# Regrouping the first casts and transposes and moving the sigmoid gates half a stage later, in a one-core recurrence and max-out kernel

## The chip, the cores and the metric

The kernel runs on one core of a Trainium2 chip. The metric is the device time of one execution in microseconds (us); several executions give a median. A profile shows one execution in detail; its "span" is about 2 us shorter than the device time of the same execution. In this kernel PE is the matrix engine, ScalarE (ACT in the profile) does sigmoids and evictions from PSUM, VectorE (DVE) the recurrence, GpSimd (POOL) issues the casting transfers, SyncE (SP) issues the transposing transfers and the stores.

## The reference, cut to what matters

```
def reference(x, f_logit, lower_bound, w1, w2, w_out):     # x: 4 x 6144 x 256
    sig = 1 / (1 + exp(-f_logit))
    f = lb + (1 - lb) * sig
    for t in range(S):                                     # recurrence over time
        h = f[:, t] * h + (1 - f[:, t]) * x[:, t];  y[:, t] = h
    y = y.reshape(24576, 256)
    return maximum(y @ w1, y @ w2) @ w_out                 # 256 -> 1024 -> 256
```

## The kernel before

The tokens are cut into 48 blocks of 512. Blocks 0 to 3 come in one by one (their "chunks" 0 to 3 are turned by PE). From then on two blocks make a pair and share one chunk of 1024 tokens: pair p uses chunk p + 2, so pair 2 uses chunk 4, pair 4 uses chunk 6. A chunk is first cast from float32 to bfloat16 into a scratch buffer in DRAM (two buffers per input, used in turn), then transposed by a transfer into on-chip memory. Each chunk has an f part and an x part.

```
def fetch(c, s):                       # cast a chunk: GpSimd issues
    nc.gpsimd.dma_start(out=scratch[s][c % NSCR], in_=src)

def cross(c):                          # transpose chunk c, then cast chunk c + 2
    for s in range(2):
        nc.sync.dma_start_transpose(out=dst, in_=scratch[s][c % NSCR])
        held[c, s] = dst
    if c + NSCR < NCHUNK:
        for s in range(2): pool_waits(held[c, s])    # GpSimd waits for the landing
        for s in range(2): fetch(c + NSCR, s)

def pair_gate(p, q):                   # one of the four sigmoids of a pair, on ScalarE
    nc.scalar.activation(out=u[:, h, cols], in_=held[c, 0][:, h, cols], func=Sigmoid)

def first_layer(j, fc):                # 2 matmuls of 512 columns into PSUM (two buffers) ...
    ...
    if fc % 2: nc.scalar.activation(out=r, in_=dT, func=Relu)   # ... evicted by ScalarE
```

The main program, cut. The place of each `pair_gate` in this text is its place in ScalarE's instruction stream:

```
for c in range(1, 6): fetch(c, 0); fetch(c, 1)        # chunks 4 and 5 among them
...
cross(4)
second_layer(0); ...
cross(5)
for fc in range(8):
    second_layer(1, fc); ...
    if fc % 2: pair_gate(2, fc // 2)                   # gates of pair 2: in front of block 2's Relus
for fc in range(8): first_layer(2, fc)
for fc in range(8):
    first_layer(3, fc); second_layer(2, fc)
    if fc % 2: pair_gate(3, fc // 2)
    ...
    if fc == 0: cross(6)
for p in range(2, 24):                                 # the stages, 16 slots each
    gates = {5: 0, 11: 1, 13: 2, 15: 3}
    for slot in range(16):
        first_layer(2 * p + slot // 8, slot % 8)       # Relu at every odd slot
        ... second layer of the pair before, vector steps of the pair after ...
        if slot == 2: cross(chunk of pair p + 3)
        if slot in gates: pair_gate(p + 2, gates[slot])
```

Of the kernel before, what the change touches and what calls it, by code (L numbers as in the profile page):

```python
# [18 lines left out]
def kernel(  # L19
# [76 lines left out]
    def fetch(c, s):  # L96
        b, t0, nt, _ = chunks[c]
        src = srcs[s][b, t0 : t0 + nt, :]
        if by_xbar(c, s):
            nc.gpsimd.dma_start(  # L100
                out=pieces(scratch[s][c % NSCR][:]), in_=pieces(src)
            )
        else:
            nat = inpool.tile([P, TB // P, D], BF16, name=("fT", "xT")[s])
            nc.gpsimd.dma_start(
                out=nat[:].rearrange("p i d -> p (i d)"),
                in_=src.rearrange("(p i) d -> p (i d)", p=P),
            )
            held[c, s] = nat
# [31 lines left out]
                    )  # L141
            raws[k, s] = dst[:].rearrange("p k i m -> p k m i")

    def cross(c):

        if c >= NCHUNK:
            return
        for s in range(2):
            dst = inpool.tile([P, KC, CH], BF16, name=("fT", "xT")[s])
            nc.sync.dma_start_transpose(out=dst[:], in_=scratch[s][c % NSCR][:])  # L150
            held[c, s] = dst
        if c + NSCR < NCHUNK:
            for s in range(2):
                pool_waits(held[c, s][:, 0, 0:1])
            for s in range(2):
                fetch(c + NSCR, s)

    def turn_steps(j):
        b, t0, nb, c, o = blocks[j]
# [50 lines left out]
    def drive(v, u, xT, cols):  # L210
        nc.vector.tensor_tensor(  # L211
            out=like(v[:, :, cols], xT), in0=like(u[:, :, cols], xT), in1=xT,
            op=ALU.mult,
        )
# [65 lines left out]
    def pair_scans(p):  # L280
        c = blocks[2 * p][3]
        new_mid(p + NBLK, ("ff", "v"))
        u, ff, v = (mids[p + NBLK, t] for t in ("u", "ff", "v"))
        for j in (2 * p, 2 * p + 1):
            ys[j] = ypool.tile([P, KC, TB], BF16, name="y")

        def driven(t):
            cols = slice(t * TB, (t + 1) * TB)
            return lambda: drive(v, u, held[c, 1][:, :, cols], cols)

        def scanned(t, h):
            return lambda: scan(2 * p + t, h, ff, v, t * TB)

        return {
            "decay": lambda: decay(ff, u, slice(0, CH)),
            "drive0": driven(0),
            "drive1": driven(1),
            **{f"scan{t}{h}": scanned(t, h) for t in range(2) for h in range(KC)},
        }
# [4 lines left out]
    om = const.tile([P, KC], FP32)  # L304
    nom = const.tile([P, KC], FP32)
    lbc = const.tile([P, KC], FP32)
    waited = const.tile([P, 1], FP32)
    warm = const.tile([P, 1], FP32)
    wob = wpool.tile([P, FC, D], BF16)
# [26 lines left out]
    def pool_waits(t):  # L336
        nc.gpsimd.tensor_copy(out=waited[:], in_=t)  # L337
# [164 lines left out]
    def sum2(p):  # L502
        sum_of(p, 2, quarter(p, 1, 1), sums[p, 3][:], ALU.subtract)
# [4 lines left out]
    def sum4(p):  # L508
        sum_of(p, 4, quarter(p, 0, 1), sums[p, 2][:], ALU.subtract)
# [106 lines left out]
    with tc.manual_schedule():  # L616
        nc.sync.dma_start(out=lbc[:], in_=lower_bound.rearrange("(h p) -> p h", p=P))
        nc.vector.tensor_copy(out=ident[:], in_=ident_f[:])
        nc.vector.tensor_scalar(
            out=om[:], in0=lbc[:], scalar1=-1.0, scalar2=1.0, op0=ALU.mult, op1=ALU.add  # L620
        )
        nc.vector.tensor_scalar_add(out=nom[:], in0=lbc[:], scalar1=-1.0)
        fetch_first(0)
        fetch_first(1)
        for g in range(NG):
            fetch_w(g)
        pool_waits(w2n[0][:, 0, 0:1])
        nc.gpsimd.dma_start(
            out=wob[:].rearrange("p (g q) c -> p g (q c)", g=NG),
            in_=moe_w_out.rearrange("(g p q) c -> p g (q c)", g=NG, q=NQ),  # L630
        )
        for c in range(1, 6):
            for s in range(2):
                fetch(c, s)
        nc.scalar.activation(out=warm[:], in_=om[:, 0:1], func=AF.Sigmoid)
        wt = ps_d.tile([P, 2, 2 * TB], BF16, name="dT")
        for q in range(8):
            nc.tensor.transpose(wt[:, 0, 0:P], ident[:], ident[:])
        first_bf16(0, 0, nc.vector.tensor_copy)
        first_bf16(0, 1, nc.vector.tensor_copy)  # L640
        first_turn(0)
        first_recurrence(0)
        first_bf16(1, 0, nc.scalar.copy)
        first_bf16(1, 1, nc.scalar.copy)
        first_turn(1)
        first_recurrence(1)
        for fc in range(2):
            make_wd(fc, 1)
        make_wd(2, 2)
        pts = [turn_w1(0), turn_w1(1)]  # L650
        for fc in range(2):
            first_layer(0, fc)
        for k in range(2):
            keep_w1T(k, pts[k])
        for fc in range(2, 4):
            first_layer(0, fc)
        make_wd(4, 2)
        make_wd(6, 2)
        pts = [turn_w1(2), turn_w1(3)]
        for fc in range(4, 8):  # L660
            first_layer(0, fc)
        for k in range(2):
            keep_w1T(2 + k, pts[k])
        make_w13()
        turn(turn_steps(1))
        recurrence(1)
        cross(4)
        for fc in range(FC):
            second_layer(0, fc)
        turn(turn_steps(2))  # L670
        gate(2)
        for fc in range(FC):
            first_layer(1, fc)
        for step in scan_steps(2):
            step()
        turn(turn_steps(3))
        gate(3)
        cross(5)
        early = scan_steps(3)
        for fc in range(FC):  # L680
            second_layer(1, fc)
            if fc < 3:
                early[fc]()
            if fc % 2:
                pair_gate(PAIR0, fc // 2)
        early[3]()
        for fc in range(FC):
            first_layer(2, fc)
        sevens = make_sevens()
        scans = pair_scans(PAIR0)  # L690
        order = [
            scans[t]
            for t in ("decay", "drive0", "scan00", "scan01", "drive1", "scan10", "scan11")
        ]
        for fc in range(FC):
            first_layer(3, fc)
            second_layer(2, fc)
            if fc % 2:
                pair_gate(PAIR0 + 1, fc // 2)
            if fc < len(order):  # L700
                order[fc]()
            if fc < len(sevens):
                sevens[fc]()
            if fc == 0:
                cross(6)

        for p in range(PAIR0, NPAIR):
            first = p == PAIR0
            more = p + 1 < NPAIR
            seq = []  # L710
            if more:
                scans = pair_scans(p + 1)
                seq += [
                    (0, scans["decay"]),
                    (10, scans["drive0"]),
                    (40, scans["scan00"]),
                    (52, scans["scan01"]),
                    (76, scans["drive1"]),
                    (84, scans["scan10"]),
                    (104, scans["scan11"]),  # L720
                    (124, lambda: sum3(p)),
                ]
            if not first:
                seq += [
                    (4, lambda: sum2(p - 1)),
                    (20, lambda: sum1(p - 1)),
                    (64, lambda: sum4(p - 1)),
                ]
            seq.sort(key=lambda e: e[0])
            steps = [] if first else sevenths(p - 1)  # L730
            done_steps = 0
            gates = {5: 0, 11: 1, 13: 2, 15: 3} if p + 2 < NPAIR else {}
            for slot in range(2 * FC):
                first_layer(2 * p + slot // FC, slot % FC)
                if first:
                    if slot % 2 == 0:
                        second_layer(2 * p - 1, slot // 2)
                upto = (slot + 1) * len(steps) // (2 * FC)
                for step in steps[done_steps:upto]:
                    step()  # L740
                done_steps = upto
                while seq and seq[0][0] < (slot + 1) * 9:
                    seq.pop(0)[1]()
                if slot == 2 and p + 3 < NPAIR:
                    cross(blocks[2 * p + 6][3])
                if slot in gates:
                    pair_gate(p + 2, gates[slot])
        for j in (NBLK - 2, NBLK - 1):
            for slot in range(FC):
                second_layer(j, slot)  # L750
# [30 lines left out]
```

## Time and profile before

| | before |
|---|---|
| device time, median of the first 3 runs | 393.57 us (392.88 to 394.91) |
| the profiled run: device time, span, mean granted clock | 398.24 us, 396.1 us, 0.987 |
| PE busy | 96% of the span |

Three lines of the page of the profiled run: busy time with share of the span and number of instructions, then the busy tenths of PE in 40 equal slices of the span, and the granted PE clock (the share of the full clock that PE was given) in tenths in the same slices.

```profile
PE 378.3 (96%) x4136; PEld 279.4 (71%) x4136; DVE 321.7 (81%) x383; ACT 288.5 (73%) x383; POOL 41.7 (11%) x98
...
PE   3997996999999999999999999999999999999996
PEclk9999698999999999999999999999999999999999
```

A slice is 9.9 us. PE has its start-up in the first slice and dips in the fourth (7) and the seventh (6); the clock row has a 6 in the fifth slice and an 8 in the seventh. Everything after that is full. So whatever can be won by moving gates or transfers lies between about 36 and 68 us.

The timeline of PE there, cut to the two instructions with a long idle time before them. Columns: start, busy time, engine, source line, operation, operands, count; in brackets the idle time of the engine just before, and what ended it.

```profile
40.57 4.42 PE L424 MATMUL dT<-y,wd 128*128 128x512 bf16 x10 [3.71 <-ACT r L432]
...
63.44 1.01 PE L424 MATMUL dT<-y,wd 128*128 128x512 bf16 x2 [3.47 <-ACT r L432]
```

PE stands 3.71 and 3.47 us, both times until a Relu (L432) frees a PSUM buffer. The timeline of ScalarE shows what was in front of these Relus:

```profile
37.42 2.19 ACT L273 ACTIVATE u<-fT 128x512 bf16<-128x512 bf16 x4 [5.57 <-DVE y L218]
39.52 1.92 ACT L432 ACTIVATE r<-dT 128x1024 bf16<-128x1024 f32 x2
...
61.84 0.63 ACT L273 ACTIVATE u<-fT 128x512 bf16<-128x512 bf16 x1 [3.63 <-DMA fT<-scr]
62.38 1.92 ACT L432 ACTIVATE r<-dT 128x1024 bf16<-128x1024 f32 x2
```

Each time a gate (L273) waited for a transposed f, and the Relu had to wait behind it. (The first wait is put down to VectorE, which had long been done; the trace has chunk 4's f landing at 37.32 us, so the transfer ended it.) The chain of waits says the same of the second of these holes (a hole is here a stretch in which PE stands idle): a 12.28 us transpose of chunk 6's f, then gate, Relu, PE.

```profile
49.46 12.28 DMA fT<-scr
61.84 0.63 ACT u L273
62.47 0.92 ACT r L432
```

Busy time of the engines in chosen stretches. Columns: stretch, its length, busy time of PE, weight load, DVE, ACT and POOL with counts, then granted clock, DMA share, GB/s. The borders are the times at which the clock changed in the trace's record, or lie whole multiples of 3.41 us from them. (The five changes of this trace after start-up are at 39.15, 45.97, 63.04, 66.45 and 397.55 us.)

```profile
35.73:39.15 3.42, 1.13 (x6) 0.39 (x4) 1.61 (x3) 1.73 (x4) 0.19 (x2) 1.00 0.71 194
39.15:42.56 3.41, 1.99 (x5) 0.69 (x5) 3.38 (x7) 2.32 (x4) 1.23 (x3) 0.50 1.78 374
42.56:45.97 3.41, 3.41 (x12) 1.58 (x11) 0.35 (x2) 2.01 (x2) 0.00 (x0) 0.50 0.78 154
59.63:63.04 3.41, 0.34 (x2) 0.06 (x1) 2.90 (x3) 1.20 (x2) 0.69 (x1) 1.00 1.08 166
63.04:66.45 3.41, 3.01 (x10) 1.47 (x10) 0.00 (x0) 1.30 (x3) 1.15 (x3) 0.50 1.13 270
```

In the stretch before each fall PE was mostly idle (1.13 and 0.34 of 3.4 us busy); then the clock is 0.50 for 6.8 us and for 3.4 us.

### The profile page before, as it was taken

The numbers are of one execution on the slowest core, as the hardware profiler recorded it, in microseconds if no ns is written. First come the engines' busy times: TensorE is split into PE (matmuls) and PEld (weight loads), VectorE is DVE, ScalarE is ACT, GpSimd is POOL, SyncE is SP. The second block draws the span as 40 slices with busy tenths as digits, with TensorE's granted clock in tenths as the row PEclk, the third lists the DMA queues.
The fourth block names the chain that finished last, engine by engine and source line by source line (L and its number), as shares of the span: only waits on it lengthen the run. The fifth ranks groups of instructions, "written<-read, shape, count | busy, mean of one in ns | idle before, by whom it ended". The sixth has DMA issues, their size and how long they took to land.

```text
span 396.1 us, 9570 instructions
## 1 busy us (share of the span) xinstructions
PE 378.3 (96%) x4136; PEld 279.4 (71%) x4136; DVE 321.7 (81%) x383; ACT 288.5 (73%) x383; POOL 41.7 (11%) x98
## 2 busy tenths in 40 slices
PE   3997996999999999999999999999999999999996
PEld 2675463777777777777777777777777777777785
DVE  5887394989889879889889889889889889889611
ACT  3654665877877887887887877877877887886750
POOL 2400111210110101100200110210210300000000
PEclk9999698999999999999999999999999999999999
DMA  7999999999999999999999999999999959320223
GB/s 255 241 244 157 186 245 257 218 199 204 248 222 91 226 156 299 211 242 205 193 238 218 253 213 162 228 242 184 216 238 183 254 69 235 126 92 18 108 84 131
DMA packets 103386, 77.17 MB, mean 195 GB/s; under 512 B 93552, under 2 KB 94064, under 8 KB 102640
## 3 DMA queue, kind: packets, MB, share of 16 engines
q1 hardware_dynamic: 100512, 51.13, 61.6%
q0 software_dynamic: 2544, 25.17, 34.0%
q8 instruction: 32, 0.52, 0.5%
q10 hardware_dynamic: 288, 0.26, 0.2%
q14 instruction: 10, 0.08, 0.1%
HBM read 53.48 MB, written 48.23 MB: 257 GB/s over the span
## 4 chain that ended last, share of the span: by engine, by line
PE 85%; DMA 3%; ACT 1%; issue 0%; DVE 0%; ACTq 0%
PE ps L602 43%; PE dT L424 39%; PE ps L471 3%; DMA fT<-scr 3%; ACT r L432 0%; ACT u L273 0%; DVE osb L480 0%; ACTq L273 0%
## 5 line engine op out<-in xcount | busy, mean ns | idle before, releaser
L432 ACT ACTIVATE r<-dT 128x1024 bf16<-128x1024 f32 x192 | 196.5, 1026 | 75.4 <-PE dT L424 74.3
L424 PE MATMUL dT<-y,wd 128*128 128x512 bf16 x768 | 229.2, 386 | 7.4 <-ACT r L432 7.4
L602 PEld LDWEIGHTS <-S 128*128 128x128 bf16 x1344 | 89.2, 98 | 34.7
L218 DVE TENSOR_TENSOR_SCAN y<-ff,y,v 128x512 bf16<-128x512 bf16 x88 | 110.2, 1274 | 0.9
L602 PEld LDWEIGHTS <-r 128*128 128x128 bf16 x1008 | 66.9, 98 | 27.3
L602 PE MATMUL ps<-t,S 128*128 128x128 bf16 x1008 | 77.0, 219 | 0.3 <-issue 0.3
L424 PEld LDWEIGHTS <-wd 128*128 128x128 bf16 x768 | 61.8, 99 | 19.0 <-issue 11.9
L273 ACT ACTIVATE u<-fT 128x512 bf16<-128x512 bf16 x88 | 54.8, 626 | 9.2 <-DVE y L218 5.6
L602 PEld LDWEIGHTS <-y 128*128 128x128 bf16 x672 | 49.6, 113 | 16.4
L493 DVE TENSOR_TENSOR S<-r 128x2048 bf16<-128x2048 bf16 x42 | 51.1, 1217 | 4.9 <-ACT r L432 4.9
L201 DVE TENSOR_SCALAR ff<-u,nom 128x1024 bf16<-128x1024 bf16 (+2 forms) x54 | 24.0, 454 | 36.3 <-ACT u L273 32.0
L493 DVE TENSOR_TENSOR S<-r,S 128x2048 bf16<-128x2048 bf16 x42 | 50.8, 1209 | 0.9 <-ACT r L432 0.9
L602 PE MATMUL ps<-wob,r 128*128 128x128 bf16 x672 | 51.2, 219 | 0.0
L560 DVE TENSOR_TENSOR osb<-ps,sn 128x512 f32<-128x512 f32 x63 | 42.9, 681 | 8.9 <-ACT r L432 5.4
L602 PE MATMUL ps<-w,y 128*128 128x128 bf16 x504 | 48.7, 219 | 0.0
L548 ACT COPY sn<-ps 128x512 f32<-128x512 f32 x63 | 37.2, 591 | 0.0
L211 DVE TENSOR_TENSOR v<-u,xT 128x1024 bf16<-128x1024 bf16 x44 | 30.1, 684 | 0.0
L337 POOL CAST waited<-fT 128x1 f32<-128x1 bf16 x20 | 7.3, 365 | 209.3 <-DMA fT<-scr 209.3
L602 PE MATMUL ps<-wob,S 128*128 128x128 bf16 x336 | 29.0, 219 | 0.0
L602 PE MATMUL ps<-t,r 128*128 128x128 bf16 x336 | 29.0, 219 | 0.0
L471 PE MATMUL ps<-wob,r 128*128 128x256 bf16 x192 | 27.1, 279 | 0.0
L471 PEld LDWEIGHTS <-r 128*128 128x128 bf16 x192 | 19.2, 100 | 4.3 <-issue 0.5
(53 smaller groups left out, 141.2 us busy)
## 6 DMA issues: line engine op xcount, KB each, us to landing
out_dram<-osb SPq DMA_DIRECT2D x47, 512.0 KB, 3.7
scr<-in_f_logit_dram POOLq DMA_DIRECT2D x22, 512.0 KB, 8.1
scr<-in_x_dram POOLq DMA_DIRECT2D x22, 512.0 KB, 10.0
r<-in_moe_w_dram SPq DMA_DIRECT2D x4, 512.0 KB, 6.4
fT<-in_f_logit_dram POOLq DMA_DIRECT2D x3, 256.0 KB, 8.0
xT<-in_x_dram POOLq DMA_DIRECT2D x3, 256.0 KB, 8.7
osb<-in_f_logit_dram SPq DMA_DIRECT2D x2, 256.0 KB, 3.2
osb<-in_x_dram SPq DMA_DIRECT2D x2, 256.0 KB, 3.6
```

Of the source, the lines that this page charges most:

```text
L201: nc.vector.tensor_scalar(out=ff[:, h, cols], in0=u[:, h, cols], scalar1=nom[:, h : h + 1], scalar2=1.0, op0=ALU.mult, op1=ALU.add,)
L211: nc.vector.tensor_tensor(out=like(v[:, :, cols], xT), in0=like(u[:, :, cols], xT), in1=xT, op=ALU.mult,)
L218: nc.vector.tensor_tensor_scan(out=ys[j][:, h, :], data0=ff[:, h, o : o + TB], data1=v[:, h, o : o + TB], initial=0.0 if t0 == 0 else ys[j ...
L273: nc.scalar.activation(out=mids[p + NBLK, "u"][:, h, cols], in_=held[c, 0][:, h, cols], func=AF.Sigmoid, scale=-1.0,)
L337: nc.gpsimd.tensor_copy(out=waited[:], in_=t)
L424: nc.tensor.matmul(dT[:, fc % 2, :], lhsT=wd[:, kc, fc * P : (fc + 1) * P], rhs=y[:, kc, :], start=(kc == 0), stop=(kc == KC - 1),)
L432: nc.scalar.activation(out=rts[j, k][:, g - 1 : g + 1, :].rearrange("p q (i m) -> p q i m", m=P), in_=dT[:].rearrange("p q (m i) -> p q i ...
L471: nc.tensor.matmul(ps[:, r, :], lhsT=left, rhs=right, start=(s == 0 and (r == 0 or j == NBLK - 1)), stop=(s == n - 1 and (r == 1 or j == N ...
L493: nc.vector.tensor_tensor(out=t[:], in0=a, in1=b, op=op)
L548: nc.scalar.copy(out=t[:], in_=bank[b][:])
L560: nc.vector.tensor_tensor(out=dst, in0=bank[b][:], in1=snap[name][:], op=ALU.add)
L602: nc.tensor.matmul(bank[b][:, i, :], lhsT=a, rhs=w, start=fresh, stop=after is not None, skip_group_check=True,)
```

## The change

Its intent: chunk 4's and 5's four casts finish first, and then their four transposes run without casts beside them; chunks 6 and 7 are each cast, then transposed, alone; from chunk 8 on two scratch buffers are in use again. The gates move: pair 2's behind block 2's Relus, and those of the stages from slots 5, 11, 13, 15 to slots 13, 15 and slots 2, 4 of the next stage. Vector steps are reordered to fit. The core of the diff, cut:

```
-    def cross(c):
+    def cross(cs, after):
+        if len(cs) > 1:                     # a tiny transfer that waits for the last cast
+            nc.sync.dma_start(out=seen[:], in_=scratch[1][cs[-1] % NSCR][CH - 1 : CH, 0:16])
+        for c in cs:
+            for s in range(2):  ... dma_start_transpose ...
         for s in range(2):
+            pool_waits(held[cs[-1], s][:, 0, 0:1])
+        for c in after:
+            if c < NCHUNK:
+                for s in range(2): fetch(c, s)
 ...
-        cross(4)
+        cross((4, 5), (6,))
 ...
-        cross(5)
         for fc in range(FC):
             second_layer(1, fc)
-            if fc % 2:
-                pair_gate(PAIR0, fc // 2)
         ... first_layer(2) ...
+        cross((6,), (7,))
         for fc in range(FC):
             first_layer(3, fc); second_layer(2, fc)
-            if fc % 2:
-                pair_gate(PAIR0 + 1, fc // 2)
-            if fc == 0: cross(6)
+            if fc < 4:
+                pair_gate(PAIR0, fc)
+            elif fc > 5:
+                pair_gate(PAIR0 + 1, fc - 6)
 ... in the stages:
-    gates = {5: 0, 11: 1, 13: 2, 15: 3}
+    gates = {2: (1, 2), 4: (1, 3), 13: (2, 0), 15: (2, 1)}     # slot: (pairs ahead, gate)
-    cross(blocks[2 * p + 6][3])
+    c = blocks[2 * p + 6][3]
+    cross((c,), (c + 1, c + 2) if first else (c + 2,))
     ... decay moved from the start of the vector steps to slot 4, scans and sums some slots later or earlier ...
```

More of the change, by code (lines that the diff above doesn't have):

```diff
@@ L142, in first_turn @@
             raws[k, s] = dst[:].rearrange("p k i m -> p k m i")
-    def cross(c):
-        if c >= NCHUNK:
-            return
-        for s in range(2):
-            dst = inpool.tile([P, KC, CH], BF16, name=("fT", "xT")[s])
-            nc.sync.dma_start_transpose(out=dst[:], in_=scratch[s][c % NSCR][:])
-            held[c, s] = dst
-        if c + NSCR < NCHUNK:
-            for s in range(2):
-                pool_waits(held[c, s][:, 0, 0:1])
-            for s in range(2):
-                fetch(c + NSCR, s)
+    def cross(cs, after):
+        if len(cs) > 1:
+            nc.sync.dma_start(
+                out=seen[:], in_=scratch[1][cs[-1] % NSCR][CH - 1 : CH, 0:16]
+            )
+        for c in cs:
+            for s in range(2):
+                dst = inpool.tile([P, KC, CH], BF16, name=("fT", "xT")[s])
+                nc.sync.dma_start_transpose(out=dst[:], in_=scratch[s][c % NSCR][:])
+                held[c, s] = dst
+        for s in range(2):
+            pool_waits(held[cs[-1], s][:, 0, 0:1])
+        for c in after:
+            if c < NCHUNK:
+                for s in range(2):
+                    fetch(c, s)
     def turn_steps(j):
@@ L282, in pair_scans @@
         new_mid(p + NBLK, ("ff", "v"))
-        u, ff, v = (mids[p + NBLK, t] for t in ("u", "ff", "v"))
+        ff, v = (mids[p + NBLK, t] for t in ("ff", "v"))
         for j in (2 * p, 2 * p + 1):
@@ L288, in driven @@
             cols = slice(t * TB, (t + 1) * TB)
-            return lambda: drive(v, u, held[c, 1][:, :, cols], cols)
+            return lambda: drive(
+                v, mids[p + NBLK, "u"], held[c, 1][:, :, cols], cols
+            )
         def scanned(t, h):
@@ L294, in pair_scans @@
         return {
-            "decay": lambda: decay(ff, u, slice(0, CH)),
+            "decay": lambda: decay(ff, mids[p + NBLK, "u"], slice(0, CH)),
             "drive0": driven(0),
@@ L306 @@
     lbc = const.tile([P, KC], FP32)
+    seen = const.tile([1, 16], BF16)
     waited = const.tile([P, 1], FP32)
@@ L692 @@
             scans[t]
-            for t in ("decay", "drive0", "scan00", "scan01", "drive1", "scan10", "scan11")
+            for t in ("drive0", "decay", "scan00", "scan01", "drive1", "scan10")
         ]
@@ L697 @@
             second_layer(2, fc)
-            if fc % 2:
-                pair_gate(PAIR0 + 1, fc // 2)
-            if fc < len(order):
-                order[fc]()
-            if fc < len(sevens):
-                sevens[fc]()
-            if fc == 0:
-                cross(6)
+            if fc < 4:
+                pair_gate(PAIR0, fc)
+            elif fc > 5:
+                pair_gate(PAIR0 + 1, fc - 6)
+            if 1 < fc:
+                order[fc - 2]()
+        scans["scan11"]()
+        for step in sevens:
+            step()
         for p in range(PAIR0, NPAIR):
@@ L713 @@
                 seq += [
-                    (0, scans["decay"]),
                     (10, scans["drive0"]),
-                    (40, scans["scan00"]),
-                    (52, scans["scan01"]),
+                    (44, scans["decay"]),
+                    (46, scans["scan00"]),
+                    (66, scans["scan01"]),
                     (76, scans["drive1"]),
@@ L724 @@
                 seq += [
-                    (4, lambda: sum2(p - 1)),
+                    (0, lambda: sum2(p - 1)),
                     (20, lambda: sum1(p - 1)),
-                    (64, lambda: sum4(p - 1)),
+                    (56, lambda: sum4(p - 1)),
                 ]
@@ L731 @@
             done_steps = 0
-            gates = {5: 0, 11: 1, 13: 2, 15: 3} if p + 2 < NPAIR else {}
+            gates = {2: (1, 2), 4: (1, 3), 13: (2, 0), 15: (2, 1)}
             for slot in range(2 * FC):
@@ L741 @@
                 done_steps = upto
+                if slot in gates:
+                    q, n = gates[slot]
+                    if p + q < NPAIR:
+                        pair_gate(p + q, n)
                 while seq and seq[0][0] < (slot + 1) * 9:
@@ L744 @@
                 if slot == 2 and p + 3 < NPAIR:
-                    cross(blocks[2 * p + 6][3])
-                if slot in gates:
-                    pair_gate(p + 2, gates[slot])
+                    c = blocks[2 * p + 6][3]
+                    cross((c,), (c + 1, c + 2) if first else (c + 2,))
         for j in (NBLK - 2, NBLK - 1):
```

## The prediction

> **What bounds the kernel now.** The page gives PE 96% busy; the chain of waits is 85% PE. In the stretches from 68 to 392 us PE is 100% busy at clock 1.00 with one 0.3 us hole; a pair of blocks takes 14.95 us. Moving casts, transposes or gates can win nothing there, only between 36 and 68 us. The list of waits has PE waiting 7.4 us for Relu evictions. The timeline shows why: a Relu stands behind a sigmoid gate that waits for a transposed chunk. Chunk 4's f lands at 37.3 us (PE resumes at 40.57 after 3.7 us); chunk 6's at 61.8 (PE resumes at 63.4 after about 3.5). After each hole the granted clock is 0.50: 39.4 to 46.2, and 63 to 66.7 us. [...] Lost to the half clock: about 2.7 + 1.7 us. At stake in all: 7.3 + 4.4, about 11.5 us.
>
> **What the change does.**
> 1. Transposes of 4 and 5 wait for all four casts, then run without casts beside them. Before, chunk 4's f took 11.4 us from issue at 25.9, because casts ran until about 31. From the last, cast-free transposes (4.2 us landing, 2.0 to 2.9 us of issue each) I estimate that the four land at about 37.5, 40, 42.5 and 45 us; chunk 5 gains some 5 us (47.1 and 51.4 before).
> 2. Gates of pair 2 move behind the Relus of block 2, so the first hole and its slow clock go. In exchange pair 2's recurrence becomes tight: gates end near 44, decay 2 x 0.48 and two scans of 1.27 us give y at about 48, while PE could want it at 46.5. I expect a new PE wait of 0.5 to 2 us.
> 3. Chunk 6's cast starts only after chunk 5 has landed (about 45 instead of 39.7), but runs alone: transposed f landing at about 55 to 57 (before 61.8). Its gate now stands at slot 13 instead of slot 5 of its stage, about 56 to 57. The second hole goes, or shrinks below 2 us.
> 4. Chunk 7 lands at about 69, needed about 71. Chunks 8 and 9 are cast together, so chunk 8's transpose meets casts again: about 86 to 89, needed about 86 to 88. A wait of 0 to 2 us is possible.
> 5. Steady stages: same instructions, other order. VectorE has about 13 us of work in 14.95. I expect PE to stay 100% busy.
>
> **Sum.** 11.5 less 1.2 (item 2) less 1.2 (items 3, 4): about 9 us. Predicted 384.5 us, 8 in 10 between 381.0 and 390.0. Faster by over 2%: 0.62; within 2%: 0.37; slower: 0.01.
>
> **What would show it.** Right: PEclk 9 in every slice after the start; PE idle between 36 and 90 us under 3 us; the chain without the 12 us transpose link; stage still 14.95 us. Wrong: gates waiting over 3 us for chunks 6, 7 or 8, with half clock behind.
>
> **What would make it wrong.** Casts and transposes in series longer than estimated (waits at chunks 6 to 8 give back 4 to 6 us); a steady stage stretched by decay coming late: 0.2 us per stage is 4 us in all.

7.3 us of waits and 4.4 (2.7 + 1.7) of half clock, "about 11.5", less 1.2 and 1.2, make about 9 us. The 2.7 + 1.7 is an estimate; half of PE's time at clock 0.50 behind each hole in the trace (40.57 to 45.97 and 63.44 to 66.45 us) comes to 2.7 + 1.5.

## The result, and the profile after

| | before | after |
|---|---|---|
| device time, median | 394.24 us (4 runs, 392.88 to 408.24) | 389.42 us (4 runs, 388.31 to 389.63) |
| the profiled run | 398.24 us, clock 0.987 | 389.44 us, clock 0.999 |

The ratio is 0.9883, 95% interval 0.9844 to 0.9923. A ratio here is the mean time of one kernel's fast runs over that of the other's of the same rounds, so it is not quite the ratio of the medians quoted. A run counts as fast when it is within 1.5% of the fastest run of the same kernel. The change is 1.2% faster: less than 2%, and half of the 9 us (2.3%) that the prediction named.

The lines of the page after that answer to those of before:

```profile
PE 370.4 (96%) x4064; PEld 278.4 (72%) x4136; DVE 320.8 (83%) x383; ACT 290.1 (75%) x383; POOL 48.1 (12%) x100
...
PE   3899999999999999999999999999999999999995
PEclk9999999999999999999999999999999999999999
```

The dips are gone and the clock is full until 386.5 us, behind the last matmul of the trace (it ends at 383.5). (72 matmul records are missing from this trace, 4064 against 4136 weight loads, so its PE busy sum is too low and is not compared.) The list of waits (total, times, longest, in us) has the Relu wait, 7.4 us before with 3.7 as the longest, at

```profile
PE dT L432 <- ACT r L440: 1.9, 5, 0.8
ACT u L278 <- DMA fT<-scr: 3.4, 2, 2.4
```

On ScalarE's timeline the Relus (now L440) of block 2 come first and the gates (now L278) behind them do not wait. The last line is the one late gate that is left, chunk 8's:

```profile
36.26 1.94 ACT L440 ACTIVATE r<-dT 128x1024 bf16<-128x1024 f32 x2 [4.18 <-PE dT L432]
38.45 1.94 ACT L440 ACTIVATE r<-dT 128x1024 bf16<-128x1024 f32 x2 [0.25 <-issue]
40.27 0.63 ACT L278 ACTIVATE u<-fT 128x512 bf16<-128x512 bf16 x1
...
90.59 0.63 ACT L278 ACTIVATE u<-fT 128x512 bf16<-128x512 bf16 x1 [2.42 <-DMA fT<-scr]
```

Because ScalarE does the 192 Relus in the same order in both kernels, the start of the first Relu of a block can be compared from trace to trace. This table has three profiled runs (starts in us); the last column is the one named "before_look3" below.

| first Relu of block | before, profiled run | after | before, a run of 394.2 us |
|---|---|---|---|
| 2 | 39.52 | 36.26 | 39.54 |
| 3 | 46.55 | 41.12 | 44.38 |
| 5 | 63.28 | 54.59 | 61.16 |
| 7 | 78.17 | 68.16 | 74.58 |
| 11 | 108.06 | 99.46 | 104.47 |
| 15 | 138.40 | 129.50 | 134.37 |
| 47 | 377.54 | 368.65 | 373.51 |

Against the profiled run of before the lead is 10.0 us at block 7, falls to 8.6 at block 11 (chunk 8's late gate) and stays 8.9. From block 15 to 47 both take 239.1 us: the steady stages are as fast as before. Against the run of 394.2 us the lead is 6.4 us at block 7 and ends at 4.9.

The same trace gives the landings of the transposed f: chunk 4 at 38.60 (37.32 before), chunk 5 at 43.73 (47.15), chunk 6 at 59.29 (61.74), chunk 7 at 72.59 (70.83), chunk 8 at 90.51 (83.36).

So the trace shows about what the prediction said it would, 8.8 us between the two profiled runs (398.24 and 389.44), and yet the medians differ by half of that. PE was idle for 7.18 us between 36 and 95 us in the profiled run of before and for 2.34 after. The experiments are about this gap.

### The profile page after: what moved, and what is told of

It is laid out like the page before. It is cut to its first block, busy times and chain, and to the rows that moved or that the text cites. A ratio compares the mean times of both kernels' runs of the same rounds, so it can differ in the third digit from the quotient of the medians.

```text
span 387.6 us, 9544 instructions
## 1 busy us (share of the span) xinstructions
PE 370.4 (96%) x4064; PEld 278.4 (72%) x4136; DVE 320.8 (83%) x383; ACT 290.1 (75%) x383; POOL 48.1 (12%) x100
## 4 chain that ended last, share of the span: by engine, by line
PE 85%; DMA 5%; DVE 4%; issue 2%; ACT 2%; SPq 0%; ACTq 0%
PE ps L610 42%; PE dT L432 36%; PE ps L479 6%; DMA fT<-scr 4%; ACT r L440 1%; DMA osb<-in_f_logit_dram 1%; DVE r L352 1%; PE ps L182 1%; DVE y L223 1%; DVE S L501 1%; DVE v L216 0%; PE ps L386 0%; DVE w1T L380 0%; DVE osb L568 0%; DVE ff L206 0%
## 5 line engine op out<-in xcount | busy, mean ns | idle before, releaser
L440 ACT ACTIVATE r<-dT 128x1024 bf16<-128x1024 f32 x192 | 196.9, 1028 | 70.2 <-PE dT L432 69.4
L432 PE MATMUL dT<-y,wd 128*128 128x512 bf16 x696 | 210.5, 381 | 4.1 <-ACT r L440 1.9
L223 DVE TENSOR_TENSOR_SCAN y<-ff,y,v 128x512 bf16<-128x512 bf16 x88 | 112.0, 1277 | 0.8
L568 DVE TENSOR_TENSOR osb<-ps,sn 128x512 f32<-128x512 f32 x63 | 42.5, 674 | 24.1 <-ACT r L440 22.2
L278 ACT ACTIVATE u<-fT 128x512 bf16<-128x512 bf16 x88 | 56.6, 644 | 3.4 <-DMA fT<-scr 3.4
L345 POOL CAST waited<-fT 128x1 f32<-128x1 bf16 x21 | 10.5, 500 | 201.4 <-DMA fT<-scr 201.4
L479 PE MATMUL ps<-wob,r 128*128 128x256 bf16 x192 | 26.2, 273 | 0.1
L206 DVE TENSOR_SCALAR ff<-u,nom 128x1024 bf16<-128x1024 bf16 (+2 forms) x54 | 22.0, 449 | 4.5 <-ACT u L200 3.9
```

The source lines that it names most:

```text
L206: nc.vector.tensor_scalar(out=ff[:, h, cols], in0=u[:, h, cols], scalar1=nom[:, h : h + 1], scalar2=1.0, op0=ALU.mult, op1=ALU.add,)
L223: nc.vector.tensor_tensor_scan(out=ys[j][:, h, :], data0=ff[:, h, o : o + TB], data1=v[:, h, o : o + TB], initial=0.0 if t0 == 0 else ys[j ...
L278: nc.scalar.activation(out=mids[p + NBLK, "u"][:, h, cols], in_=held[c, 0][:, h, cols], func=AF.Sigmoid, scale=-1.0,)
L345: nc.gpsimd.tensor_copy(out=waited[:], in_=t)
L432: nc.tensor.matmul(dT[:, fc % 2, :], lhsT=wd[:, kc, fc * P : (fc + 1) * P], rhs=y[:, kc, :], start=(kc == 0), stop=(kc == KC - 1),)
L440: nc.scalar.activation(out=rts[j, k][:, g - 1 : g + 1, :].rearrange("p q (i m) -> p q i m", m=P), in_=dT[:].rearrange("p q (m i) -> p q i ...
```

## The experiments

Theory A: the profiled run of before was not a typical run. It contains two half-clock stretches that most runs don't have, so the prediction took a gain read in a run of 398 us off a median of 393.6 us. Rival B: the half clock is the rule, and something in the changed kernel gives 4 us back. Rival C: casts and transposes that overlap land at different times from run to run, so that the holes themselves differ.

In all there were 12 runs, in three groups. The kernels of a group shared a chip and the runs of before. Before's times in these groups were: 11 runs 390.01 to 426.1, median 396.32; 11 runs 391.65 to 414.53, median 395.31; 13 runs 391.95 to 409.83, median 396.09. The medians below are over all runs, slow ones too: before's times run from 390.0 to 401.0 us with no gap over 1.3 us, so the line of 1.5% cuts through the middle of them. Where the ratio of fast runs says something else, it is given.

### 1. before_again: the unchanged kernel

No edit.

> The unchanged kernel once more, for its spread. Theory A (the first profile of before was not typical: its granted clock fell to 0.50 in two stretches, 10.2 us in all, and its span of 396.1 us is some 4.4 us longer than a median run of 393.6 us would give): most runs here have a mean granted clock near 1.00 and spans near 391.5 to 392.5, a few have 0.987 and about 396; a profile at clock 1.00 shows the same two holes of PE (3.7 and 3.5 us) at full clock behind them. Rival B (the profile was typical, and the profiling adds some 4 us to before but not to after): all runs show 0.985 to 0.99. Rival C (the landings of the transposes differ from run to run): a profile here shows the second hole shorter, chunk 6's f landing well before 61 us.

Six runs: 391.15, 392.89, 395.61, 396.84, 398.87, 403.93, with mean granted clocks of 0.998, 0.999, 0.995, 0.993, 0.987, 0.983. The profiled one is that of 396.84, and its PE timeline has other holes than the first profile:

```profile
40.83 3.90 PE L424 MATMUL dT<-y,wd 128*128 128x512 bf16 x10 [3.78 <-ACT r L432]
...
71.44 0.56 PE L602 MATMUL ps<-t,S 128*128 128x128 bf16 x7 [1.79 <-DVE S L493]
...
105.97 0.66 PE L602 MATMUL ps<-t,S 128*128 128x128 bf16 x9 [1.92 <-ACT sn L548]
```

The first hole is there, with one half-clock stretch of 3.41 us behind it (the mean clock is 0.83 from 35 to 45 us and 1.00 from 45 to 57). The second is not: chunk 6's f landed at 54.5 us, but its x only at 69.5 (63.6 in the first profile), and the waits came later. So C holds for the landings. Of the clocks neither A nor B had it right: A wanted most of them near 1.00, and of these six runs and the eleven of before beside them four have 0.998 or more; B wanted all at 0.985 to 0.99, and three lie there.

### 2. keep_warm: spare matmuls in the two holes of before

```
+    def idle_work(j, n):                           # nobody reads the result
+        spare = ps_o.tile([P, 2, D], FP32, name="ps")
+        for q in range(n): nc.tensor.matmul(spare, lhsT=wd[:, 0, 0:P], rhs=ys[j][:, 0, :], ...)
 ...
+            if fc == 4: idle_work(2, 12)          # in front of first_layer(2, 4)
+                if first and slot == 10: idle_work(4, 12)
```

> Before, with 12 spare matmuls (about 2.6 us) put where PE stands in each of its two holes: after four slices of the first layer of block 2, and before slot 10 of pair 2. The result is unchanged. Theory A (half clock is rare): no slow clock, and the same time as the median of before within 0.5 us. Rival B (half clock is the rule): the clock stays at 1.00 and the time falls by 3 to 4.5 us, to about 389.5 to 390.5.

Six runs: 391.85, 392.57, 398.12, 399.03, 407.98, 412.47; the profiled one (392.57) had a full clock. Its two holes were filled: the longest idle stretch of PE between 36 and 95 us is 0.3 us. As a test of A against B this is inconclusive: the spread is far larger than either effect. It does show that the spread does not come from the half clock alone, since three runs have a mean clock of 1.000, at 391.85, 392.57 and 398.12 us. The question is asked again in experiments 9 and 10 on a kernel with steady landings.

### 3. gates_only: new gates, old casts and transposes

```
-        cross((4, 5), (6,))          +        cross(4)   ...   cross(5)
-        cross((6,), (7,))            +            if fc == 0: cross(6)
-        cross((c,), ...)             +        cross(blocks[2 * p + 6][3])   # casts chunk c + 2, as before
```

> The later gates and the new order of the vector steps, but casts and transposes as before (4, 5, 6 one by one, two scratch buffers from the start). If the gates carry the gain: both holes gone or under 1 us, chunk 6's f at about 62 us needed at about 57 so that a wait of some 3 us stays at slot 13, and the time 2 to 4 us below before. If the pairing of casts and transposes carries it: no gain over 1 us.

Median 389.67 (389.24 to 394.18), against a median of 396.32 of before beside it: a larger gain than expected. The printed ratio is 0.9941 only because before's fastest run was 390.01, so that its runs from 396.23 up were not counted as fast; seven of its eleven runs were left out. The wait of 3 us that was expected for chunk 6's f did not come; PE stood for 1.87 us in front of 66.72 us instead, behind chunk 6's x (landed at 64.75). The late gates, with the vector steps reordered to fit them, reach the time of the whole change without the new casts; the two were not tried apart.

### 4. dma_only: new casts and transposes, old gates

```
-        cross(4)                     +        cross((4, 5), (6,))
-        cross(5)                     (removed)
-            if fc == 0: cross(6)     +        cross((6,), (7,))               # before that loop
-        cross(blocks[2 * p + 6][3])  +        cross((c,), (c + 1, c + 2) if first else (c + 2,))
```

> The new casts and transposes, but gates and vector steps at the old places. Chunk 4's f then lands near 38.5 instead of 37.3 and its gate still stands in front of the Relus of block 2: the first hole grows by about 1 us. Chunk 6's f lands near 59 instead of 61.7, so the second hole shrinks by about 2 us less the later start. If the gates carry the gain: within 1.5 us of before, and both holes still there. If the grouping carries it: 3 us or more below before.

Median 399.89 (398.6 to 400.83), ratio 1.0178 [1.0127, 1.0230]: slower, by less than 2%. All six runs have a clock of 0.982 to 0.987. The first hole is 4.70 us here. Both holes of before were expected; the second is gone, since chunk 6's f landed at 56.48. In its place a hole that the expectation missed comes at chunk 8, whose f landed at 90.06: chunk 9's casts run beside its transpose (experiment 7 tests that this is the cause). PE and ScalarE there:

```profile
91.30 1.12 PE L608 MATMUL ps<-t,S 128*128 128x128 bf16 x9 [4.20 <-ACT sn L554]
```

```profile
90.14 0.63 ACT L278 ACTIVATE u<-fT 128x512 bf16<-128x512 bf16 x1 [4.79 <-DMA fT<-scr]
```

So the two parts of the change don't add up: with early gates the new casts cost about 3.6 us against the median of before, with late gates they cost or give nothing that shows beside gates_only.

### 5. after_again: the changed kernel

No edit.

> The changed kernel unaltered, on one chip with the three below and with before. Theory (landings are steady where casts and transposes don't overlap): median 388.5 to 390, spread under 2 us, chunk 6's f landing within 1.5 us of 59.3; before beside it spreads over more than 5 us.

Six runs, 389.1 to 391.34, median 389.57; before beside it 391.65 to 414.53, median 395.31. The spread is 2.2 us and chunk 6's f landed at 57.36, both a little outside what was expected. The ratio was 0.9876 [0.9826, 0.9926].

### 6. gates_again: gates_only a second time

No edit against gates_only.

> New gates with old casts and transposes, a second time, for its spread beside the changed kernel. If the gates carry the gain: median within 1 us of the changed kernel. If the grouping of casts adds safety: more spread than the changed kernel, single runs 2 us or more slower. If the grouping costs time: faster than the changed kernel by 0.5 us or more.

Median 389.8, beside 389.57 of the changed kernel: the same; the ratios to before are 0.9880 and 0.9876. The spread is 5.1 us (388.21 to 393.3) against 2.2, as expected if the grouping adds safety. Its profiled run (391.06) shows what a single unlucky landing does. Chunk 6's x landed at 65.3 us, VectorE had waited 2.38 us for it, and the sum that PE needed stood behind that step. PE stood for 2.28 us, and the clock fell after it (1.00 from 64.02 to 67.43 us, with PE busy for 1.14 of these 3.41; the mean from 60 to 75 us is 0.89):

```profile
67.24 0.78 PE L604 MATMUL ps<-t,S 128*128 128x128 bf16 x7 [2.28 <-DVE S L495]
```

### 7. always_alone: every later chunk cast only after the one before has been transposed

```
-                    cross((c,), (c + 1, c + 2) if first else (c + 2,))
+                    cross((c,), (c + 1,))
```

> The changed kernel, but every later chunk too is cast only after the one before it has been transposed, never two at a time. If the hole of PE of 1.0 us at 90 us comes from chunk 9's casts running into chunk 8's transposes: chunk 8's f lands near 86 instead of 90.5, the hole goes, and the time falls by about 1 us, to some 388.3. If one chunk at a time is too slow in the steady stages (13.3 us a chunk measured at chunk 7, against 14.95 us of a stage): later holes, and 1 us or more slower.

Six runs, 387.94 to 389.09, median 388.08; ratio to before 0.9834 [0.9791, 0.9878]. It is faster than the changed kernel on the same chip by 1.5 us, and no run of the one reaches into the range of the other, if only just (389.09 is its slowest, 389.1 is the changed kernel's fastest). It beats both kernels. What the expectation named as the reason shows in the trace: chunk 8's f landed at 86.33 instead of 90.33, and its gate no longer waits (compare the 2.42 us of after):

```profile
88.40 0.62 ACT L278 ACTIVATE u<-fT 128x512 bf16<-128x512 bf16 x1
```

After start-up this trace has no hole of PE over 0.9 us. The transfers' medians from issue to landing (last number of each line), first in before, then in this kernel:

```profile
scr<-in_f_logit_dram POOLq DMA_DIRECT2D x22, 512.0 KB, 8.1
scr<-in_x_dram POOLq DMA_DIRECT2D x22, 512.0 KB, 10.0
...
fT<-scr SPq DMA_TRANSPOSE x22, 12.1
xT<-scr SPq DMA_TRANSPOSE x22, 9.7
```

```profile
scr<-in_f_logit_dram POOLq DMA_DIRECT2D x22, 512.0 KB, 5.6
scr<-in_x_dram POOLq DMA_DIRECT2D x22, 512.0 KB, 8.4
...
fT<-scr SPq DMA_TRANSPOSE x22, 5.6
xT<-scr SPq DMA_TRANSPOSE x22, 4.6
```

With transfers one after the other, the median transpose took 5.6 and 4.6 us here, about half of the 12.1 and 9.7 us in before, where casts overlap them. A chunk's round, from landing to landing of its x, was 13.9 us from chunk 7 to 8 (74.33 to 88.23), which still fits into a stage of 14.95 us.

### 8. early_slots: the changed kernel with the stages' gates at the old slots

```
-            gates = {2: (1, 2), 4: (1, 3), 13: (2, 0), 15: (2, 1)}
+            gates = {5: (2, 0), 11: (2, 1), 13: (2, 2), 15: (2, 3)}
+            if first: gates |= {2: (1, 2), 4: (1, 3)}
```

> The changed kernel with the gates of the steady stages back at slots 5, 11, 13 and 15 (pair 2's and 3's stay late), to see what the half stage is worth under the new casts. Chunk 6's f (about 59.3) is then wanted at about 52: a hole of some 4 us; chunk 8's (about 90) at about 83: a hole of some 3 to 5 us more. Time 394 to 398. If the half stage is not needed: within 1 us of the changed kernel.

Median 398.69 (395.43 to 407.75), 9.1 us slower than the changed kernel and just above the range that was expected; its ratio to before is 1.0083 [1.0022, 1.0144]. Both expected holes are there:

```profile
59.68 0.59 PE L432 MATMUL dT<-y,wd 128*128 128x512 bf16 x2 [4.69 <-ACT r L440]
...
91.03 1.12 PE L610 MATMUL ps<-t,S 128*128 128x128 bf16 x9 [2.43 <-ACT sn L556]
```

The half stage is what hides chunks 6 and 8 under the new casts. The spread is 12.3 us here and 2.2 in after_again, although the casts and transposes are the same: how far the landings show in the time depends on where the gates stand.

### 9 and 10. pair2_early and pair2_warm: the first hole by itself, with and without spare matmuls

Base: always_alone. In pair2_early only pair 2's gates go back in front of block 2's Relus; pair2_warm adds 14 spare matmuls in the hole (3.19 us of PE in its trace).

```
             second_layer(1, fc)
+            if fc % 2: pair_gate(PAIR0, fc // 2)
...
-            if fc < 4: pair_gate(PAIR0, fc)
...                                                  # pair2_warm only:
+            if fc == 4: idle_work(2, 14)            # in front of first_layer(2, 4)
```

> The one-chunk-at-a-time kernel (388.1 us), with pair 2's four gates alone put back in front of block 2's Relus, so that the first hole comes back by itself with steady landings. Chunk 4's f lands near 38.4: PE should stand from about 37 to 41 (about 4 us), the clock should then fall to 0.50 for 3.4 us or more. Theory (hole plus half clock): 5 to 7 us slower, 393 to 395. If the first hole is made up later by waits that were there anyway: under 2 us slower.

> The kernel above with 14 spare matmuls (about 3 us) in the hole, so that PE idles about 1 us instead of 4. Theory (the half clock costs half of its length): the clock stays at 1.00 and the time is 1.7 to 3.4 us less than the kernel above. If the half clock costs nothing that counts, or the spare work itself delays: within 0.7 us of it or slower.

pair2_early: median 393.67, and all six runs lie within 0.7 us, 5.6 us above always_alone. pair2_warm: median 392.36 (392.15 to 392.95). PE's timeline, first of pair2_early, then of pair2_warm:

```profile
41.48 4.00 PE L432 MATMUL dT<-y,wd 128*128 128x512 bf16 x10 [4.48 <-ACT r L440]
```

```profile
41.70 1.94 PE L432 MATMUL dT<-y,wd 128*128 128x512 bf16 x8 [1.72 <-ACT r L440]
```

The stretches of 3.41 us there, two of pair2_early and one of pair2_warm (columns and borders as before):

```profile
38.13:41.54 3.41, 0.06 (x1) 0.06 (x1) 0.69 (x1) 3.21 (x6) 0.00 (x0) 1.00 1.16 239
41.54:44.96 3.42, 3.42 (x9) 1.24 (x9) 0.00 (x0) 1.82 (x2) 0.18 (x1) 0.50 1.12 178
```

```profile
39.13:42.54 3.41, 1.70 (x8) 0.68 (x7) 0.69 (x1) 3.41 (x6) 0.00 (x0) 1.00 1.13 226
```

The clock fell to 0.50 for 3.41 us in the first and stayed at 1.00 in the second. The hole costs 4.3 us (392.36 less 388.08), and the half clock 1.3 us more (393.67 less 392.36). (The spare matmuls hardly delay the work behind the hole: it starts at 41.70 us with them and at 41.48 without.) The 1.3 us are a little under half of the 3.41 us stretch, and below the 1.7 that was expected. With steady landings the half clock is thus a real cost, and the granted clocks say that it happened in all six runs of pair2_early (0.993 to 0.996, against 0.997 to 1.000 in pair2_warm).

### 11 and 12. before_look2 and before_look3: two more profiles of the unchanged kernel

No edit, one execution each.

> A third profile of the unchanged kernel. Theory (overlapping casts and transposes land where luck puts them, so holes move and the clock falls after some): the first hole is there again near 37 to 40.5, chunk 6's f lands anywhere from 52 to 62 us, and the later holes are at other places than in the first two profiles. Rival (two kinds of run, each always the same): it repeats one of the two profiles within 1 us.

> A fourth profile of the unchanged kernel, same expectations as the third. A run under 393 us should show no half clock after block 4 and at most one later hole.

They took 393.3 and 394.23 us. Neither fell to the half clock before its last matmuls. look2 has chunk 4's f early (34.97 us) and holes of 1.38, 1.59 and 3.24 us. look3 is the telling one: it repeats the two holes of the first profile (against the expectation that the later holes would move), chunk 4's f landing at 37.34 and chunk 6's at 59.62. The expectation for a run under 393 us was not tried, since both are above it.

```profile
40.59 1.94 PE L424 MATMUL dT<-y,wd 128*128 128x512 bf16 x8 [3.69 <-ACT r L432]
...
61.31 0.59 PE L424 MATMUL dT<-y,wd 128*128 128x512 bf16 x2 [3.20 <-ACT r L432]
```

```profile
PE   3997897999999999999999999999999999999996
PEclk9999999999999999999999999999999999999999
```

The same holes, to 0.3 us, but the clock row is full and the run is 4.0 us shorter than the first profiled run (394.23 against 398.24). What can be compared is PE's idle time in stretches of 3.41 us. Their borders in look3 are an estimate: they lie whole multiples of 3.41 us before the clock change at the end of the same trace, as the changes of the first trace do. The hole from 36.90 to 40.59 is cut in two by such a border, and the second hole lies across one at 59.27:

```profile
35.37:38.79 3.42, 1.53 (x8) 0.59 (x6) 1.99 (x3) 1.34 (x3) 0.18 (x1) 1.00 0.62 154
38.79:42.20 3.41, 1.61 (x8) 0.72 (x8) 3.02 (x6) 3.16 (x5) 1.23 (x3) 1.00 1.75 393
...
59.27:62.68 3.41, 1.36 (x9) 0.87 (x9) 1.13 (x1) 2.46 (x3) 0.63 (x1) 1.00 0.90 118
```

PE was idle for 55%, 53% and 60% of these. In the first profile the hole of the same length lay so that one stretch was idle for 67% (1.13 of 3.42 us busy), and the clock fell at its end; in its second hole a stretch was idle for 90% (0.34 of 3.41 us busy), and it fell there too.

## Why the prediction was wrong, point by point

The step that failed is the first sum: "At stake in all: 7.3 + 4.4, about 11.5 us", taken with "Lost to the half clock: about 2.7 + 1.7 us" from one profiled run, and then subtracted from the median of other runs. The profiled run took 398.24 us; the median that the 9 us were taken off was 393.57, 4.7 us less. Every sign that the prediction named under "Right" came: a full clock row, 1.45 us of idle PE between 36 and 90 us, no transpose of 12 us in the chain (though one of 10.46, chunk 8's), and stages of 14.95 us. So the mechanism was right, and one term of the sum was mis-sized.

The holes were sized rightly. PE's idle time between 36 and 95 us is 7.18 us in the first profile, 7.29 in look3 and 2.34 after: 4.9 us less, which is the prediction's 7.3 less 2.4, and look3 is 4.9 us behind the changed kernel at block 47.

The half clock was not. look3 has the same two holes, no half clock behind them, and is 4.0 us shorter than the first profile; 3.6 us of that are there by block 7, just behind the two slow stretches. So the half clock was worth about 3.6 us in the run in which it was read, and nothing in look3. The baseline of 393.57 less the 389.42 of the changed kernel is 4.15 us, no more than the holes alone: **the mis-sized term is the 4.4 us of half clock, of which about nothing was left in the median that it was subtracted from.** That the three runs behind this median had little half clock is inferred from this sum, since their clocks are not on record; twelve later runs of before between 392.88 and 394.92 us have a median clock of 0.996.

How common is the half clock in before? The mean clock is on record for 43 further runs of it. It is 0.997 or more in 9, 0.993 to 0.996 in 15, 0.989 to 0.991 in 13, and 0.987 (as in the first profile) or less in 6; the median is 0.994. A stretch of 3.41 us at 0.50 takes 0.004 off the mean (half of 3.41 of 396.1 us), and the slow end of the kernel up to 0.003 (after_again has a mean of 0.997, and 1.00 from 30 to 130 us; look2 and look3 have 0.998), so I estimate about one stretch in a typical run, against three (10.2 us) in the first profile. Theory A as it was put (most runs near 1.00) is therefore wrong; what holds of it is that the profiled run had more half clock than most. Of Rival B it holds that some half clock is the rule; but nothing in the changed kernel gives 4 us back (from block 15 on both kernels take the same 239.1 us), and profiling does not add 4 us, since look2 and look3 were profiled too. Rival C holds as a source of before's wide spread, which is there at full clock too.

There was bad luck in the baseline as well: the median of all 47 runs of before (without the first profile) is 395.6 us, and the three runs that gave 393.57 were 2.0 us quicker. As an estimate, 395.6 less 4.9 for the holes less 1.3 for one half-clock stretch (its cost in pair2_early) is 389.4 us, and the changed kernel took 389.42. With a typical baseline the 9 us would still have been some 3 us too much.

The other points:

1. "the four land at about 37.5, 40, 42.5 and 45 us": late by 1.1 to 1.3 us (38.60, 41.23, 43.73, 46.34). The last cast landed at 33.75 (32.57 before).
2. "the first hole and its slow clock go": right. Of the "new PE wait of 0.5 to 2 us" for pair 2's scans nothing showed: the list of waits has no PE wait for VectorE there.
3. Chunk 6's f "landing at about 55 to 57": 59.29 in the first profile of the changed kernel, 57.36 in the second, so late by up to 2.3 us. In the first its gate waited 0.96 us and PE 0.34; "shrinks below 2 us" was right.
4. "so chunk 8's transpose meets casts again": right, but later than said (90.51 instead of 86 to 89). The gate waited 2.42 us, and PE 0.84 us before the matmul at 92.19 that the Relu behind it released. The time is within the "0 to 2 us" of the prediction. always_alone takes the cause away: from block 9 to 15 it took 44.84 us, after_again 45.91, so 1.1 us of its 1.5 us come from here; the rest was not traced.
5. "I expect PE to stay 100% busy" in the steady stages: right, 14.95 us each.
6. The chances (0.62 for over 2%) leaned the wrong way for the same reason. Even against before's 395.6 us, the 389.4 us are 1.6% faster, still within 2%.

Which part does the work: the late gates, with the vector steps reordered to fit. gates_only reaches 389.7 without the new casts; the new casts without the late gates lose 3.6 us. The overlapping casts of chunk 8 and after even cost 1.5 us, as always_alone shows. The spread narrows when both parts are in: 2.2 us in after_again, 5.1 in gates_again (old casts), 12.3 in early_slots (early gates), 12.8 us and more in every group of runs of before. It is narrowest where every chunk is cast alone, 0.7 to 1.2 us in always_alone, pair2_early and pair2_warm. These are ranges of six runs each, so rough.

What stays open: why overlapping casts and transposes land at different times from run to run (chunk 6's f landed anywhere from 52.8 to 61.7 us in seven profiles with the old casts), and what the slowest runs of before (405 to 426 us) ran into; no profile caught one.

Whether a hole was followed by the half clock did not go by its length in these runs. Holes of 3.71 and 3.47 us (first profile), 2.28 us (gates_again) and 2.43 us (early_slots, mean clock 0.91 from 75 to 95 us) were; holes of 3.69 and 3.20 us (before_look3) were not. In the first trace the clock fell 2.3 and 3.1 us after PE had gone idle. Of the stretches of 3.41 us looked at, PE was idle for 67% and 90% (first profile), 67% (gates_again) and 98% (pair2_early) of those that the clock fell after, and for 50% (pair2_warm) and 53 to 60% (before_look3) of those that it stayed full after; some of these borders are estimates, and what decides was not shown. But a hole of 3.7 us cost a half clock in one run of the kernel and none in another, so a prediction should have weighted it, not added it in full.

## What to carry to other kernels

Before taking a gain read in a profile off a median, compare the device time of the profiled run with that median; here they were 4.7 us apart, half of the predicted gain. Look at the clocks of several runs before counting a half clock that one profile shows. Where an engine evicts for the bottleneck, put its work on late-arriving data behind the evictions and as late as its consumers allow: half a stage turned holes of 4.7 and 2.4 us (early_slots) into holes of 0.3 and 0.8 us. And let transfers that slow each other run one after the other when the round still fits into the stage; that was 1.5 us faster and made the time steady, with less overlap and not more.
